# Five exchanges in a load queue: a v ahead of a q, and k and v ahead of weight blocks

## The chip, the cores and the metric

The kernel runs on one core of one Trainium2 chip. The metric is the device time of one execution in microseconds (us), taken as the median of several executions. A profiled execution gives a trace beside it. The engines of the core are called as in the profile: PE is TensorE (matrix products, with PEld for its weight loads), DVE is VectorE, ACT is ScalarE, POOL is GpSimd, and SP is SyncE, which here issues nearly all DMAs. PE writes into PSUM banks, DVE and ACT read them, and loads land in SBUF.

## The reference

Two stages follow each other. The first is a linear attention with decay, over 4 batches, 8 heads, 768 positions and a head dimension of 64, in blocks of 64 positions:

```python
intra = np.einsum('bhic,bhjc->bhij', qb, kb) * Dmask[None]
intra = np.einsum('bhij,bhjd->bhid', intra, vb)
inter = np.einsum('bhid,bhde->bhie', qb * lam_pow[None], kv_state)
out[:, :, sl] = intra + inter
kb_dec = kb * rev_pow[None]
kv_state = lam_block[None, :, None, None] * kv_state + np.einsum('bhsd,bhse->bhde', kb_dec, vb)
```

Its output, with the heads side by side, is x, 3072 tokens by 512. The second stage is a pair of products with a leaky activation between them; w_in is 512 x 2048 and w_out is 2048 x 512, both given as 64-bit floats:

```python
h = x @ w_in
g = np.maximum(0.01 * h, h)
return (g @ w_out).astype(np.float32)
```

## The kernel before

**Tiling.** The attention goes in 24 chunks of 128 positions (two blocks of the reference each), six to a batch, numbered 0 to 23 here. For a chunk c the kernel loads kc, qc and vc (`load_kq`, line 476, and `load_v`, line 538). A k or a q is two DMAs of 128 KB, a v one of 256 KB. All three have 256 bytes in a piece, one head of one position. PE transposes k and q with four products each (`transposes`, line 560), ACT or DVE copies the result out of PSUM (line 541), and POOL or DVE multiplies k by the decay (line 601). PE then makes the products of k and v (`kv` in `scores`), which renew the state, the scores (`go` in `scores`), and the output in three parts (`outputs`: `own`, then `inter(0)` and `inter(1)`). All of these are 64 x 64 products with line 420. Between the two `inter` parts stands a copy of two columns (`seen_po`, line 692), which orders them. The output goes to x in a split into three float32r parts: xh (line 708), xl (716) and xm (734).

For chunks 8 and 9 q isn't transposed on PE. It is loaded in 16 small pieces (`load_subs`, line 523, 32 KB each) into a buffer that DVE transposes (`turn`, line 532); DVE must have all 16 pieces first.

**Weights.** w_in goes in eight blocks of 256 columns. Each block is loaded in two halves of 512 KB (`to_float32`, line 797, called W below) into one of three buffers raw0 to raw2. ACT reads a half three times (lines 809, 811 and 813), DVE makes float32 of it (815, 816), and ACT or DVE splits the block into three parts wh, wm and wl (`parts`, 822, 825, 827). `up` (line 863) multiplies four chunks of x with a block, three products for the three parts; ACT applies the activation (890), and the result is stored to a buffer G in device memory (893). After all 24 chunks, `down` (929) reads G and multiplies with w_out.

**What sets the order.** A planner records every operation with a number, in the order in which Python calls come. `ORDER` (line 266) is a list written out in full: pairs of an operation's number and its engine. It fixes the order in which each engine gets its operations, 1,291 of 1,841 of them; the planner places the others behind the list by its own times. Each engine runs its own list strictly in order, so an operation that waits holds all that stand behind it on that engine; for SP this means all DMAs behind a waiting one.

```python
for i, e in self.order:
    if i < 0:
        done.append((free[e], len(done), i, e))
        free[e] -= 0.11 * i
        continue
    take(max(free[e], since(i, e)), i, e)
```

PSUM banks for an operation are handed out in the same order: `Slot("bank")` gets, of the banks pt, b10, b11 and b2 that are free at that point of the list, the one that was used last the longest ago (`resolve`):

```python
able = [x for x in self.kinds[s.kind] if holds[x] is None or not holds[x].left]
s.name = self.kinds[s.kind][s.fixed] if s.fixed is not None else min(able, key=lambda x: ended[x])
```

So moving an operation of PE can rename banks behind it. Which buffer a load writes is fixed by the chunk: even chunks use k0, q0, v0 and odd ones k1, q1, v1, so a load of chunk c + 2 waits until chunk c has been read. Chunks 2 and 3 have places of their own (k and v of 2 in gs0, of 3 in gs1, q of 3 in raw2).

The operations that this case speaks of:

| number | what | engine |
|---|---|---|
| 51 | load of v2 | SP |
| 73 | load of q3 (two DMAs, into raw2) | SP |
| 76 | transposes of q3 | PE |
| 59 | products of k2 and v2 | PE |
| 230, 224 | second and first half of w_in block 3 | SP |
| 135, 162, 121, 187 | load of k6, store of a part of G, load of v5, load of q7 | SP |
| 331 | second half of w_in block 4 | SP |
| 154 | load of v6 | SP |
| 268, 281, 280, 278 | four of the 16 pieces of q for chunks 8 and 9 | SP |
| 275 | the last of these pieces | SP |
| 208, 283, 303 | loads of v7, k8 and v8 | SP |
| 304 | load of k9 (two DMAs) | SP |
| 355 | second half of w_in block 7 | SP |

Of the kernel before, what the change touches and what calls it, by code (L numbers as in the profile page):

```python
# [239 lines left out]
def kernel(  # L240
# [127 lines left out]
    plan = Plan(kinds, also, {"k@2": early[0], "v@2": early[0], "k@3": early[1], "v@3": early[1], "q@3": early[2]})  # L368
    plan.fill, plan.idle, plan.warm, plan.order = busy, None if ORDER else busy, 1.3 + 0.22 * WARM, ORDER
    add = plan.add  # L370
# [685 lines left out]
```

## Time and profile before

| what | value |
|---|---|
| median of 3 runs | 607.72 us (606.0 to 608.35) |
| the profiled execution | 606.76 us, its span 605.0 us |
| busy, share of the span: PE | 597.4 us, 99% |
| DVE, ACT, POOL | 295.6 us (49%), 209.0 us (35%), 71.4 us (12%) |
| granted TensorE clock | 1.000 |
| DMA, mean over the span | 174 GB/s |

A row of the timeline reads: start in us from the span's start, length, engine, line, operation, written tile <- read tiles, partitions x elements, number of instructions merged into the row, and in brackets the idle time ahead of it with what ended that. Tiles go by the program's names: `att` is the common buffer of the attention's k, q, v and states, `raw` a weight half, `b`, `pt`, `po` and `psc` are PSUM banks, `gs` the staging of G. SPq rows are issues of DMAs; their length is that of the issue and not of the transfer. An issue that lasts longer than about half a microsecond was held while the queue took it in.

### The profile page before, as it was taken

To read this page: it belongs to the slowest core of one execution; us is meant where nothing else is said; L and a number is where in the kernel's file an instruction comes from. 1 tells how busy PE (TensorE), PEld (TensorE's weight loads), DVE (VectorE), ACT (ScalarE), POOL (GpSimd) and SP (SyncE) were. 2 spreads that over 40 slices of the span, in tenths; PEclk is the share of its full clock that TensorE was granted. 3 is DMA by queue.
4 is the path that set the end of the run, shared out by engine and by line. 5 is a ranking of instruction groups with operands and counts; after the bars stand their busy time and mean duration, and the time that the engine had idled before them with its cause. 6 is when DMAs were issued, how large, how long until landed. Compare 5 with 4: busy or idle time off the path is not lost.

```text
span 605.0 us, 12719 instructions
## 1 busy us (share of the span) xinstructions
PE 597.4 (99%) x5362; PEld 492.9 (81%) x5362; DVE 295.6 (49%) x410; ACT 209.0 (35%) x322; POOL 71.4 (12%) x85
## 2 busy tenths in 40 slices
PE   8899999999999999999999999999999999999997
PEld 6788888888888888887888888888888888888886
DVE  6898754350454434344166755354353543534430
ACT  3776651212433433435334421222312313214111
POOL 3321232241322031140000000000000000000000
PEclk9999999999999999999999999999999999999999
DMA  9998887598888788664875833424333333433201
GB/s 211 226 264 223 216 246 199 89 251 191 215 227 206 226 240 243 174 205 178 326 262 183 304 105 126 153 94 137 117 117 127 117 128 122 125 102 123 86 1 69
DMA packets 149993, 105.18 MB, mean 174 GB/s; under 512 B 125872, under 2 KB 126640, under 8 KB 149936
## 3 DMA queue, kind: packets, MB, share of 16 engines
q1 hardware_dynamic: 149648, 104.30, 59.5%
q8 instruction: 42, 0.69, 0.5%
q14 instruction: 15, 0.12, 0.1%
q10 hardware_dynamic: 288, 0.07, 0.0%
HBM read 68.69 MB, written 35.65 MB: 172 GB/s over the span
## 4 chain that ended last, share of the span: by engine, by line
PE 95%; DMA 3%; ACT 1%; issue 0%; DVE 0%; POOL 0%; SPq 0%; DVEq 0%; POOLq 0%; ACTq 0%
PE b L863 32%; PE b L929 16%; PE psc L929 11%; PE po L929 11%; PE pt L863 11%; PE pt L929 5%; PE po L420 4%; PE psc L420 3%; DMA att<-in_v_dram 1%; DMA att<-in_k_dram 1%; PE b L359 1%; DMA raw<-in_moe_w_in_dram 1%; PE b L560 1%; PE b L420 0%; PE pt L359 0%
## 5 line engine op out<-in xcount | busy, mean ns | idle before, releaser
L911 DVE SCALAR_TENSOR_TENSOR xl<-att,xh 128x1024 fp32r<-128x1024 f32 x48 | 58.7, 1222 | 125.8 <-ACT xh L910 125.8
L910 ACT ACTIVATE xh<-att 128x1024 fp32r<-128x1024 f32 x48 | 50.9, 1061 | 147.5 <-PE po L929 72.9
L863 PE MATMUL b<-xl,wl 128*128 128x512 f32 (+1 forms) x292 | 77.1, 389 | 0.0
L863 PE MATMUL b<-xh,wh 128*128 128x512 f32 (+1 forms) x292 | 76.5, 389 | 0.6 <-ACT wh L822 0.6
L863 PE MATMUL b<-xm,wm 128*128 128x512 f32 (+1 forms) x292 | 75.9, 390 | 0.0
L890 ACT ACTIVATE gs<-b 128x512 f32<-128x512 f32 x72 | 42.1, 597 | 94.8 <-PE b L863 86.3
L863 PEld LDWEIGHTS b<-xh,wh 128*128 128x128 f32 x292 | 53.9, 188 | 11.8 <-ACT wh L822 0.7
L863 PEld LDWEIGHTS b<-xl,wl 128*128 128x128 f32 x292 | 54.1, 188 | 11.2
L863 PEld LDWEIGHTS b<-xm,wm 128*128 128x128 f32 x292 | 53.8, 188 | 11.2
L913 DVE SCALAR_TENSOR_TENSOR xm<-xl,xh 128x1024 fp32r<-128x1024 f32 x48 | 58.8, 1226 | 4.7
L929 PE MATMUL b<-wh,xh 128*128 128x512 f32 x144 | 56.0, 389 | 0.0
L929 PE MATMUL b<-wl,xl 128*128 128x512 f32 x144 | 56.0, 389 | 0.0
L929 PE MATMUL b<-wm,xm 128*128 128x512 f32 x144 | 56.0, 389 | 0.0
L663 POOL TENSOR_TENSOR att<-att 128x256 f32<-128x256 f32 x40 | 28.0, 701 | 112.6 <-DVE att L660 59.9
L929 PE MATMUL psc<-wm,xm 128*128 128x512 f32 (+1 forms) x100 | 38.2, 387 | 0.0
L929 PE MATMUL po<-wm,xm 128*128 128x512 f32 (+1 forms) x100 | 37.9, 384 | 0.0
L929 PE MATMUL psc<-wh,xh 128*128 128x512 f32 x96 | 37.3, 389 | 0.0
L929 PE MATMUL psc<-wl,xl 128*128 128x512 f32 x96 | 37.3, 389 | 0.0
L929 PE MATMUL po<-wh,xh 128*128 128x512 f32 x96 | 37.3, 389 | 0.0
L929 PE MATMUL po<-wl,xl 128*128 128x512 f32 x96 | 37.3, 389 | 0.0
L420 PEld LDWEIGHTS po<-att 64*64 64x64 f32 x1408 | 26.9, 134 | 10.2 <-issue 8.2
L420 PE MATMUL po<-att 64*64 64x64 f32 x1408 | 33.0, 222 | 1.4 <-issue 0.9
(106 smaller groups left out, 863.9 us busy)
## 6 DMA issues: line engine op xcount, KB each, us to landing
att<-g SPq DMA_DIRECT2D x48, 512.0 KB, 3.4
g<-gs SPq DMA_DIRECT2D x47, 512.0 KB, 3.6
raw<-in_moe_w_in_dram SPq DMA_DIRECT2D x16, 512.0 KB, 5.9
raw<-in_moe_w_out_dram SPq DMA_DIRECT2D x16, 512.0 KB, 4.5
out_dram<-gs SPq DMA_DIRECT2D x23, 256.0 KB, 2.0
att<-in_k_dram SPq DMA_DIRECT2D x44, 128.0 KB, 3.9
att<-in_v_dram SPq DMA_DIRECT2D x22, 256.0 KB, 4.2
wo<-w SPq DMA_DIRECT2D x8, 512.0 KB, 4.3
```

The lines of the kernel that those rows point to most:

```text
L359: nc.tensor.matmul(wide[:, :k, :], lhsT=ident, rhs=_bc(ident[:, 0:C2], 1, k), start=True, stop=True, skip_group_check=True)
L420: nc.tensor.matmul(dst[HALF[cols]], lhsT=lhsT[HALF[rows]], rhs=rhs[HALF[rows]], start=start, stop=True, skip_group_check=True)
L560: nc.tensor.transpose(out=at[y], in_=src[:, 2 * y:2 * y + 2, :].rearrange("p a d -> p (a d)"), identity=ident)
L663: add("POOL", 0.62, lambda new=new, j=j: behind(("s", j), nc.gpsimd.tensor_tensor(state[(j + 1) % 4], new, _bc(lam_c, 2, D), op=ALU.mult)) ...
L863: nc.tensor.matmul(dst, lhsT=w[z][:, kk * 2 * P + f * P:kk * 2 * P + (f + 1) * P], rhs=x[z][:, kk, toks], start=start and kk == 0, stop=kk ...
L890: add("ACT", ns, lambda b=b, r=r: nc.scalar.activation(out=r(), in_=b(), func=AF.Prelu, bias=0.0, scale=1.0, alpha=0.01), [kb], [kg], rank ...
L910: add("ACT", 1.05, lambda: nc.scalar.activation(out=h, in_=graw[j], func=AF.Copy, bias=0.0, scale=NEAR), reads, wr("h"))
L911: add("DVE", 1.215, lambda: nc.vector.scalar_tensor_tensor(l, graw[j], 1.0, h.bitcast(F32), op0=ALU.mult, op1=ALU.subtract), reads + [f"rh ...
L913: add("DVE", 1.215, lambda: nc.vector.scalar_tensor_tensor(m, l.bitcast(F32), -S, h.bitcast(F32), op0=ALU.mult, op1=ALU.add), [f"rh{j}", f ...
L929: nc.tensor.matmul(to[:, cols], lhsT=ring[j][z][:, f * T + tb * P:f * T + (tb + 1) * P], rhs=W[pp][z][:, f * d_model:(f + 1) * d_model][:, ...
```

## The change

`ORDER` alone changes. Seen from the queue of SP there are five exchanges; on PE operation 76 moves behind 59. In the diff, other entries of the list are left out where the line is only "...", and each pair of lines is one place of the list.

```diff
-    (38, "DVE"), (73, "DMA"), (37, "DVE"),
+    (38, "DVE"), (37, "DVE"),
...
-    (51, "DMA"), (97, "ACT"), (104, "ACT"), (96, "ACT"), (171, "DMA"),
+    (51, "DMA"), (97, "ACT"), (104, "ACT"), (96, "ACT"), (73, "DMA"), (171, "DMA"),
...
-    (155, "PE"), (76, "PE"), (47, "DVE"), (77, "ACT"), (60, "DVE"), (59, "PE"), (65, "PE"),
+    (155, "PE"), (47, "DVE"), (77, "ACT"), (60, "DVE"), (59, "PE"), (76, "PE"), (65, "PE"),
...
-    (230, "DMA"), (135, "DMA"), (162, "DMA"),
+    (135, "DMA"), (162, "DMA"),
...
-    (187, "DMA"), (137, "PE"), (139, "PE"), (224, "DMA"),
+    (187, "DMA"), (137, "PE"), (139, "PE"), (230, "DMA"), (224, "DMA"),
...
-    (245, "PE"), (331, "DMA"), (232, "ACT"),
+    (245, "PE"), (232, "ACT"),
...
-    (234, "DVE"), (228, "DVE"), (271, "DMA"),
+    (234, "DVE"), (228, "DVE"), (331, "DMA"), (271, "DMA"),
...
-    (325, "DMA"), (268, "DMA"), (236, "DVE"), (281, "DMA"), (196, "ACT"), (201, "DVE"), (208, "DMA"),
-    (250, "PE"), (199, "ACT"), (261, "PE"), (204, "DVE"), (251, "ACT"), (280, "DMA"), (237, "DVE"), (278, "DMA"), (334, "ACT"), (283, "DMA"),
+    (325, "DMA"), (236, "DVE"), (196, "ACT"), (201, "DVE"), (208, "DMA"),
+    (250, "PE"), (199, "ACT"), (261, "PE"), (204, "DVE"), (251, "ACT"), (237, "DVE"), (334, "ACT"), (283, "DMA"),
...
-    (326, "ACT"), (267, "DMA"),
+    (326, "ACT"), (268, "DMA"), (281, "DMA"), (280, "DMA"), (278, "DMA"), (267, "DMA"),
...
-    (355, "DMA"), (304, "DMA"),
+    (304, "DMA"), (355, "DMA"),
```

1. The load of v2 goes ahead of the load of q3 (two DMAs). The transposes of q3 on PE go behind the products of k2 and v2, and the banks pt, b10 and b11 change names for the operations behind, up to the end of `up`; the order of the operations on PE, DVE, ACT and POOL is otherwise the same.
2. The second half of w_in block 3 goes behind the loads of k6, v5 and q7 and a store of G, six DMAs in all, to just ahead of that block's first half.
3. The load of v6 goes ahead of the second half of w_in block 4.
4. Four pieces of q go behind the loads of v7 and k8.
5. The load of k9 goes ahead of the second half of w_in block 7.

2 lines of the change are left out of this document (1 added, 1 removed).

## The prediction

> **What bounds the kernel now.** I read the page's first part, then the busy time by stage, then the timeline of TensorE and of the load queue in the first 70 us.
>
> ```profile
> span 605.0 us, 12719 instructions
> ...
> PE 597.4 (99%) x5362; PEld 492.9 (81%) x5362; DVE 295.6 (49%) x410; ACT 209.0 (35%) x322; POOL 71.4 (12%) x85
> ```
> ```profile
> 0.00:69.44 69.44, 65.34 (x1267) 52.60 (x1267) 55.70 (x104) 42.39 (x73) 19.14 (x29) 1.00 0.93 229
> 69.44:600.00 530.56, 530.52 (x4093) 439.03 (x4088) 239.10 (x305) 165.98 (x248) 52.24 (x56) 1.00 0.56 167
> ```
>
> In the stage rows the columns are the stage, its length and then the busy time of PE, weight loads, DVE, ACT and POOL, with the granted clock, the DMA share and the GB/s last. The reader is to see that TensorE (PE) is busy for 530.52 of 530.56 us from 69.44 on, at clock 1.00. All edits lie ahead of that. Behind it the work is the same and PE is full, so the change is worth as many microseconds as PE reaches the place now at 69.44 earlier or later. Ahead of it PE idles 69.44 - 65.34 = 4.1 us. That caps a gain at about 4 us, while a loss has no cap in these rows. The DMA engines are 0.93 busy in that stage, so the load queue is the second resource that matters.
>
> **The change part by part.** No instruction is added or removed. Five groups of issues change places in SyncE's queue (SP), the four transposes of q3 change places with the products of k2 and v2 on PE, and PSUM banks pt, b10 and b11 change names among the same uses. For the banks I take 0: each new owner still waits for a reader that ended earlier on ACT or DVE. A letter with a number is a chunk's load (v5), W is half a block of w_in.
>
> *First exchange, v2 ahead of q3.*
>
> ```profile
> 15.13 1.05 SPq L476 DMA_DIRECT2D raw<-in_q_dram  x2
> 16.23 0.51 SPq L538 DMA_DIRECT2D gs<-in_v_dram  x1
> ```
> ```profile
> 20.89 0.60 PE L560 MATMUL pt<-att,raw 128*128 128x128 f32 x4
> 21.59 0.69 PE L420 MATMUL b<-gs 64*64 64x64 f32 x32
> ...
> 23.75 0.46 PE L420 MATMUL po<-att 64*64 64x64 f32 x16
> ```
> ```profile
> 22.95 0.70 ACT L809 ACTIVATE w<-raw 128x512 f32<-128x512 f32 x1 [0.84 <-DMA raw<-in_moe_w_in_dram]
> 23.55 0.14 ACT L692 COPY att<-po 128x2 f32<-128x2 f32 x1
> ```
>
> v2 is issued 16.23 - 15.13 = 1.1 us earlier, q3 0.5 us later (v's issue of 0.51). The products, at 21.59 today, can follow their predecessor at 20.89, 0.7 us earlier, and the transposes (0.60) follow them. But the last part of this chunk's output, at 23.75, needs the small copy at 23.55 on ACT, and that stands behind an operation that waits for a W until 22.95. That W keeps its place. So PE is early and then waits: 0 gained from 23.75 on. If v2 is no earlier, 0 lost; if W is late too, up to 0.7 lost. I take 0.
>
> *Second, W (block 3) behind k6, the store of G01, v5 and q7 (six DMAs).*
>
> ```profile
> 31.56 0.46 SPq L797 DMA_DIRECT2D raw<-in_moe_w_in_dram  x1
> 33.52 0.92 SPq L476 DMA_DIRECT2D att<-in_k_dram  x2
> 35.19 0.59 SPq L538 DMA_DIRECT2D att<-in_v_dram  x1
> 35.84 3.50 SPq L476 DMA_DIRECT2D att<-in_q_dram  x2
> 39.43 0.74 SPq L797 DMA_DIRECT2D raw<-in_moe_w_in_dram  x1
> ```
> ```profile
> 39.39 0.73 PE L560 MATMUL po<-att 128*128 128x128 f32 x4
> ...
> 41.32 1.09 PE L420 MATMUL psc<-att 64*64 64x64 f32 x46 [0.35 <-DMA att<-in_v_dram]
> ```
> ```profile
> 41.47 0.81 ACT L811 ACTIVATE low<-raw 128x512 uint16<-128x512 uint32 x1
> 42.80 0.60 ACT L708 ACTIVATE xh<-po 128x512 fp32r<-128x512 f32 x1 [0.52 <-PE po L420]
> ...
> 45.91 0.79 ACT L811 ACTIVATE low<-raw 128x512 uint16<-128x512 uint32 x1 [0.83 <-DMA raw<-in_moe_w_in_dram]
> ```
>
> k6 waits for the chunk 4 products and can't be issued before 33.52 in either order. What changes is that 512 KB of W no longer lie ahead of it. v5 then lands ahead of W, and the 0.35 us wait at 41.32 goes. The four transposes of k6 take 0.73 where those of q3 above take 0.60, another 0.13. W goes out at 39.43 - 2.5 (the issue of q7 shrinks from 3.50 to about 1) = 36.9 instead of 31.56, and lands between 36.9 + 4.2 = 41.1 (the time that the W of 60.37 below takes) and 36.9 + 6.5 = 43.4 (that of the W of 39.43, which ACT gets at 45.91); I take 42. Its reader on ACT, at 41.47, waits about 0.6 us, and the next in that queue, xh at 42.80, slips to about 43. The bank that xh empties is next written by the transposes of k7, whose load is issued only behind the products at 41.32, so I take 0 for that. Gain 0.35 + 0.13 = 0.48 us; ends 0 (W still shares the engines) and 0.6.
>
> *Third, v6 ahead of a W (block 4); fourth, four pieces of transposed q behind v7 and k8.*
>
> ```profile
> 57.80 0.80 PE L560 MATMUL po<-att 128*128 128x128 f32 x4
> ```
>
> The third gains 0: PE follows without a wait today, and v6 comes 0.5 us earlier in issue; it keeps the products covered when PE comes early. The fourth brings k8 four issues forward. Its transposes take 0.80 against 0.60, so 0.20 us gained. The pieces only have to be there for the DVE transposes at 67.22 below.
>
> *Fifth, k9 (two DMAs) ahead of a W (block 7).*
>
> ```profile
> 60.37 0.40 SPq L797 DMA_DIRECT2D raw<-in_moe_w_in_dram  x1
> 60.87 0.96 SPq L476 DMA_DIRECT2D att<-in_k_dram  x2
> 61.89 0.49 SPq L523 DMA_DIRECT2D att<-in_q_dram  x1
> 62.43 0.44 SPq L538 DMA_DIRECT2D att<-in_v_dram  x1
> ```
> ```profile
> 66.59 0.68 PE L560 MATMUL po<-att 128*128 128x128 f32 x4 [0.33 <-DMA att<-in_k_dram]
> 67.20 0.93 PE L420 MATMUL po<-att 64*64 64x64 f32 x48
> 67.95 1.32 PE L420 MATMUL psc<-att 64*64 64x64 f32 x64
> 69.09 0.41 PE L420 MATMUL po<-att 64*64 64x64 f32 x16
> ```
> ```profile
> 67.22 1.30 DVE L532 STREAM_TRANSPOSE att<-att 128x512 f32<-128x512 f32 x2 [2.25 <-DMA att<-in_q_dram]
> ```
> ```profile
> 64.53 0.67 ACT L809 ACTIVATE w<-raw 128x512 f32<-128x512 f32 x1 [0.66 <-DMA raw<-in_moe_w_in_dram]
> 65.74 0.74 ACT L813 ACTIVATE low<-raw 128x512 f16<-128x512 f32 x1
> 68.20 0.16 ACT L692 COPY att<-po 128x2 f32<-128x2 f32 x1 [1.71 <-PE po L420]
> ```
>
> k9 is issued at most 0.5 us earlier and has 512 KB less ahead of it: the wait of 0.33 goes, and 0.08 of the transposes (0.68 against 0.60). It waits for the chunk 7 products that read the same buffer, and may have to wait for them, so up to 0.5 of the earlier issue can be lost unless PE is early; the W, the q piece and v8 are now queued behind that wait. Gain 0.41.
>
> The PE-side sum is 0 + 0.48 + 0 + 0.20 + 0.41 = 1.1 us. It isn't kept whole, because other work is late next at the same place. (a) The last q piece, issued at 61.89, releases the DVE transposes at 67.22; their second one ends at 67.22 + 1.30 = 68.5, and the scores of chunk 8, the second half of the 64 at 67.95, need it. (b) v8, issued at 62.43, is read by the first half at 67.95. (c) W moves behind 256 KB of k and two issues (0.96), so it lands between 64.5 + 1.0 = 65.5 and 66.8; its three operations on ACT take 65.74 + 0.74 - 64.53 = 1.95 us and stand ahead of the small copy at 68.20, for which the last 16 products at 69.09 wait. The copy could start at 67.5 to 68.8. All three go by when the queue has drained, which moves the same bytes in either order. If that time stays, 0 of the 1.1 us is kept. It may come earlier, because the load of k7 waits for the chunk 5 products, which come 0.5 us earlier, and because k9 fills a stretch in which the queue starves:
>
> ```profile
> 60.40:62.00 1.60, 1.60 (x71) 1.45 (x64) 1.57 (x2) 1.14 (x3) 0.00 (x0) 1.00 0.60 62
> 62.00:66.00 4.00, 4.00 (x19) 3.17 (x17) 2.60 (x5) 3.34 (x7) 2.27 (x3) 1.00 1.03 260
> ```
>
> 62 GB/s against 260 is 1.6 x 198 = 317 KB, or 1.2 us at 260 GB/s; an estimate from these two rows. Between 0 and 1.1 I take half, 0.5 us. So the span becomes 605.0 - 0.5 = 604.5 us. The profiled execution took 606.76 us, its span and 1.76 around it; like that, 606.3. It lay 0.96 below the median of 607.72, and the mean of the four executions (607.72, 608.35, 606.0, 606.76) is 607.2. Minus 0.5 that is 606.7, and from the median 607.2; I forecast the middle, 607.0.
>
> **A rule weighed.** In these rows loads end in the order of their issue: W of 60.37 lets ACT go at 64.53, k9 of 60.87 lets PE go at 66.59. The Trainium skill, "DMA: Bandwidth & Descriptors", section "Queues, rings and completion order", says that descriptors are consumed in ring order on each engine, but that completion is not first in, first out for an issuing engine. By the first half the exchanges move the landings, as summed; were landings free of the order, no wait would go, and the time would be rival one's. The trace agrees with the first half.
>
> **The rivals.** *One: hidden anyway.* The waits go, but PE stands at the scores of chunk 8 until 68.5 as today, because (a) keeps its time. For it: the DVE row waits 2.25 us for a load. Against it: the starved stretch. Time: span 605.0, median 607.7.
>
> *Two: slower, W holds ACT.* W of block 7 lands late, and the small copy behind it holds PE. It decides from the point where W lands later than 69.09 - 0.16 - 1.95 = 67.0. A W in the crowded stretch is slower than this one: the W at 39.43 releases ACT only at 45.91 (row above, 6.5 us), and one of 6.5 us issued at 61.4 lands at 67.9, 0.9 us beyond the point; with a wait of 0.7 of its own in the first exchange, 1.6. Span 606.6, time 609.3. Against it: W took 64.53 - 60.37 = 4.2 us here.
>
> *Three: all is kept.* The queue drains 1.2 us earlier, and PE keeps 1.1: span 603.9, time 606.6 from the median.
>
> **How the numbers follow.** Forecast (0.2 to 0.9 us off) 0.45, rival one 0.25, rival two 0.18, rival three 0.12. A measurement of this kernel tells about 0.5% from no change, 3.0 us; the three runs shown spread over 2.35 us. No case reaches 3.0 us by its mechanism, so what lies beyond is the spread of the medians and a stall that I don't see: 0.04 faster, 0.06 slower, 0.90 within. The range takes rival three less 1.2 us of the runs' spread at the low end, 605.4, and rival two without its own spread at the high end, 609.3.
>
> **What would show it.** Right: no PE wait on a v or k load between 30 and 68 us; v5, k8 and k9 landing earlier; PE's last 16 products of chunk 7 starting at 68.2 to 68.9 instead of 69.09, with a DVE or ACT wait just ahead; and the stage behind as full as now. Wrong: new PE waits ahead of 69 us on ACT's small copy or on the DVE transposes, k9's issue held by the chunk 7 products, or any PE idle time behind 70 us.

## The result, and the profile after

The changed kernel takes 609.28 us (median of 22 executions, 606.42 to 613.73) against 606.94 us for the kernel before (22 executions). The ratio is 1.0041, with a 95% interval of 1.0029 to 1.0054. A second measurement of the same two kernels gave 1.0054 (1.0036 to 1.0073). So the change costs 2.3 to 3.3 us. The time lies inside the range and within half a per cent, as forecast, but the forecast had the sign wrong: it said 0.5 us faster. Single executions of 850 to 2,104 us (one each of e2, e6 and e12 below, and one of the kernel before) are left out of all medians and counts.

The traced execution is the shortest of the 22 (606.42 us), so its trace alone does not show the loss; what the others do is read below from repeats and from neighbours of this kernel. Busy time by stage, of the changed kernel (columns as in the prediction):

```profile
span 604.6 us, 12718 instructions
```
```profile
0.00:69.39 69.39, 64.60 (x1266) 51.72 (x1267) 55.24 (x104) 41.95 (x73) 19.09 (x29) 1.00 0.92 231
69.39:600.00 530.61, 530.61 (x4095) 439.09 (x4090) 238.89 (x305) 165.87 (x248) 51.84 (x56) 1.00 0.56 167
```

The place that was at 69.44 is now at 69.39, and behind it PE is as full as before. Timeline of PE, the changed kernel:

```profile
39.96 1.05 PE L420 MATMUL psc<-att 64*64 64x64 f32 x46
...
56.61 0.87 PE L560 MATMUL po<-att 128*128 128x128 f32 x4 [0.19 <-DMA att<-in_k_dram]
...
65.25 0.60 PE L560 MATMUL po<-att 128*128 128x128 f32 x4
65.78 0.93 PE L420 MATMUL po<-att 64*64 64x64 f32 x48
67.89 1.34 PE L420 MATMUL psc<-att 64*64 64x64 f32 x64 [1.18 <-DMA att<-in_v_dram]
69.05 0.41 PE L420 MATMUL po<-att 64*64 64x64 f32 x16
```

PE seems to come early as summed: the products of v5 start at 39.96 (41.32 before) without a wait, and the transposes of k9 at 65.25 (66.59 before), 1.34 us earlier. Then 1.18 us go into a new wait for v8, whose products start at 67.89, where they started before (67.95). But the 1.34 us are no larger than what one kernel differs by from trace to trace. A second trace of the kernel before (e2 below, an execution of 605.17 us) has none of the waits that the prediction added up:

```profile
40.42 1.05 PE L420 MATMUL psc<-att 64*64 64x64 f32 x46
...
56.73 0.60 PE L560 MATMUL po<-att 128*128 128x128 f32 x4
...
65.10 0.74 PE L560 MATMUL po<-att 128*128 128x128 f32 x4
```

The products of v5 start between 39.89 and 41.32 in the six traces without the second exchange and between 39.96 and 41.49 in the fourteen with it; the mean is 40.57 in both. So no gain on PE is shown; the new wait for v8 is what stays. Timeline of SyncE's queue, the changed kernel:

```profile
51.69 5.35 SPq L523 DMA_DIRECT2D att<-in_q_dram  x5
57.14 0.40 SPq L893 DMA_DIRECT2D g<-gs  x1
57.58 3.32 SPq L523 DMA_DIRECT2D att<-in_q_dram  x6
61.01 1.67 SPq L476 DMA_DIRECT2D att<-in_k_dram  x2
62.77 0.46 SPq L797 DMA_DIRECT2D raw<-in_moe_w_in_dram  x1
63.28 0.46 SPq L523 DMA_DIRECT2D att<-in_q_dram  x1
63.79 0.44 SPq L538 DMA_DIRECT2D att<-in_v_dram  x1
64.33 0.52 SPq L893 DMA_DIRECT2D g<-gs  x1
```

Two rows of the same view of the kernel before:

```profile
57.00 3.27 SPq L523 DMA_DIRECT2D att<-in_q_dram  x6
...
62.98 3.03 SPq L893 DMA_DIRECT2D g<-gs  x1
```

Six small pieces stood in a row before, from 57.00 on; five more now stand in front of them, and only the store of G00 lies between, from 51.69 to 60.90. v8 is issued at 63.79 instead of 62.43, though PE needs it 1.2 us sooner. The store of G02 behind v8 took 3.03 us to issue before, which I read as a full queue ahead of it; now it takes 0.52, which fits an empty one. By this reading the holds have moved ahead of v8. Stretches of 5 us, the kernel before and the changed one:

```profile
55.00:60.00 5.00, 5.00 (x55) 3.76 (x55) 3.69 (x8) 3.20 (x5) 0.31 (x1) 1.00 0.81 207
60.00:65.00 5.00, 5.00 (x108) 4.30 (x101) 4.57 (x7) 3.48 (x7) 1.96 (x3) 1.00 0.88 202
```
```profile
55.00:60.00 5.00, 4.79 (x123) 3.56 (x123) 3.46 (x7) 3.35 (x6) 0.62 (x1) 1.00 0.61 159
60.00:65.00 5.00, 5.00 (x38) 3.81 (x28) 4.24 (x6) 2.82 (x5) 1.86 (x3) 1.00 0.59 119
65.00:70.00 5.00, 3.82 (x137) 3.19 (x136) 2.55 (x5) 2.43 (x5) 1.46 (x2) 1.00 1.08 345
```

The last two columns tell it: from 55 to 65 the DMA engines are 0.6 busy instead of 0.8 to 0.9 and move (207 - 159 + 202 - 119) x 5 = 655 KB less, which has to be made up behind 65. At 345 GB/s that is 1.9 us, an estimate from these rows. Here too the trace matters: e2's trace of the kernel before moves 159 and 217 GB/s, so it is 490 KB against that one, all of it between 60 and 65.

A second sign stands in the executions themselves. The mean granted clock of PE was 1.000 in 9 of the 22 and 0.993 to 0.997 in 13. The 9 average 608.0 us, the 13 average 610.5, the kernel before 607.0. A clock of 0.997 over 607 us would be 1.8 us, an estimate.

### The profile page after: what moved, and what is told of

Read it like the earlier page. It is cut to its first block, busy times and chain, and to the rows that moved or that the text cites. A ratio compares the mean times of both kernels' runs of the same rounds, so it can differ in the third digit from the quotient of the medians.

```text
span 604.6 us, 12718 instructions
## 1 busy us (share of the span) xinstructions
PE 596.4 (99%) x5362; PEld 491.9 (81%) x5362; DVE 294.9 (49%) x410; ACT 208.4 (34%) x322; POOL 70.9 (12%) x85
## 4 chain that ended last, share of the span: by engine, by line
PE 94%; DMA 3%; DVE 1%; ACT 1%; issue 0%; SPq 0%; DVEq 0%; ACTq 0%
PE b L863 31%; PE b L929 16%; PE pt L863 12%; PE psc L929 11%; PE po L929 11%; PE pt L929 5%; PE po L420 4%; PE psc L420 3%; DMA raw<-in_moe_w_in_dram 1%; DMA att<-in_v_dram 1%; DMA g<-gs 1%; PE b L560 1%; DMA att<-in_lam_dram 0%; PE po L560 0%; DVE att L403 0%
## 5 line engine op out<-in xcount | busy, mean ns | idle before, releaser
L863 PE MATMUL b<-xl,wl 128*128 128x512 f32 (+1 forms) x288 | 75.1, 387 | 0.0
L863 PE MATMUL b<-xh,wh 128*128 128x512 f32 (+1 forms) x288 | 74.5, 385 | 0.6 <-ACT wh L822 0.6
L890 ACT ACTIVATE gs<-b 128x512 f32<-128x512 f32 x70 | 40.7, 596 | 84.4 <-PE b L863 71.7
L863 PEld LDWEIGHTS b<-xl,wl 128*128 128x128 f32 x288 | 52.7, 188 | 11.1 <-DVE wl L827 0.4
L863 PEld LDWEIGHTS b<-xm,wm 128*128 128x128 f32 x288 | 52.5, 188 | 10.8
```

The costliest lines, as they stand in the source:

```text
L863: nc.tensor.matmul(dst, lhsT=w[z][:, kk * 2 * P + f * P:kk * 2 * P + (f + 1) * P], rhs=x[z][:, kk, toks], start=start and kk == 0, stop=kk ...
L890: add("ACT", ns, lambda b=b, r=r: nc.scalar.activation(out=r(), in_=b(), func=AF.Prelu, bias=0.0, scale=1.0, alpha=0.01), [kb], [kg], rank ...
```

## The experiments

Three theories were put to the chip. A: PE idles, its clock falls for a while, and that is the loss. B: the loads land late, and the clock is a by-product. C, formed after the first four runs, says why they are late: the small pieces of q are bound by SyncE's issue. Each ratio is to the kernel before, measured beside it on the same chip. "Low clock" counts executions with a mean clock under 0.998.

| run | kernel | median us | ratio (95%) | low clock |
|---|---|---|---|---|
| e1 | changed, again | 609.85 | 1.0054 (1.0036 to 1.0073) | 3 of 6 |
| e2 | before, again | 606.15 | 0.9997 (0.9985 to 1.0010) | 0 of 11 |
| e3 | without 1 | 611.79 | 1.0072 (1.0047 to 1.0097) | 6 of 7 |
| e4 | without 5 | 608.75 | 1.0047 (1.0031 to 1.0063) | 8 of 12 |
| e5 | without 4 | 607.07 | 1.0004 (0.9992 to 1.0017) | 0 of 12 |
| e6 | 4 alone | 607.63 | 1.0011 (0.9994 to 1.0028) | 3 of 11 |
| e7 | changed + 2 fillers | 608.95 | 1.0041 (1.0023 to 1.0059) | 2 of 9 |
| e8 | changed, W early | 606.76 | 0.9994 (0.9984 to 1.0004) | 0 of 11 |
| e9 | 3 and 4 | 607.01 | 1.0011 (0.9996 to 1.0027) | 3 of 12 |
| e10 | 2 and 4 | 607.89 | 1.0012 (0.9996 to 1.0028) | 1 of 12 |
| e11 | changed, 4 pieces on ACT | 606.04 | 0.9987 (0.9973 to 1.0002) | 0 of 12 |
| e12 | without 4, 4 pieces on ACT | 608.71 | 1.0031 (1.0014 to 1.0048) | 2 of 11 |
| e13 | 2, 3 and 4 | 608.35 | 1.0035 (1.0020 to 1.0050) | 3 of 8 |
| e14 | before, 4 pieces on ACT | 605.78 | 0.9990 (0.9977 to 1.0003) | 0 of 12 |
| e15 | changed, ACT and W early | 606.49 | 0.9994 (0.9979 to 1.0008) | 0 of 12 |
| e16 | 1 alone | 605.86 | 1.0000 (0.9986 to 1.0014) | 0 of 12 |
| e17 | changed + 4 fillers | 609.54 | 1.0057 (1.0039 to 1.0075) | 0 of 9 |
| e18 | e11 again | 606.58 | 1.0006 (0.9988 to 1.0024) | 1 of 12 |

**Both kernels again (e1, e2).** No edit.

> The changed kernel once more, unchanged, for a trace of a typical execution: the traced one took 606.42 us, 2.9 below its median of 609.28. In 13 of its 22 executions the mean granted clock of TensorE was 0.993 to 0.997, in 9 it was 1.000; the first group averages 610.3 us, the second 608.0. Theory A, the clock: a thin stretch of TensorE work ahead of 70 us makes the clock drop for a few us; 0.0035 of 605 us is 2.1 us. Then a trace with a mean clock under 1 shows one stretch ahead of 75 us with a granted clock of 0.5 to 0.9 and nothing else behind, and the ratio is again 1.003 to 1.005. Theory B, late landings: the clock is a by-product, v8, the last q piece or the W of block 7 lands 2 to 3 us later than in the trace at hand, and the wait of 1.2 us at 66.6 is 3 to 4 us.

> The kernel before once more, unchanged, for its clock execution by execution. Theory A: 1.000 in all or nearly all executions, ratio 0.999 to 1.001, 606.9 us. Theory B: executions under 1.000 are as common here as in the changed kernel (about 6 in 10) and cost it nothing that sets the two apart.

The loss is there again, and the kernel before is itself again with no low clock. Of all executions of the kernel before that ran beside these experiments and have a clock on record, 4 of 140 are low; of the changed kernel, 16 of 28. So the clock belongs to the change. But it is not all: the changed kernel's executions at a full clock are still 1.0 us slower than the kernel before (608.0 against 607.0). The trace of e1 has no stretch with a lower clock ahead of 75 us and took 607.9 us; its starved stretch and its wait for v8:

```profile
60.00:65.00 5.00, 5.00 (x126) 4.39 (x126) 4.34 (x6) 3.08 (x6) 1.84 (x4) 1.00 0.59 129
```
```profile
69.26 1.45 PE L420 MATMUL psc<-att 64*64 64x64 f32 x64 [1.20 <-DMA att<-in_v_dram]
```

The same picture: a starved queue and a wait of 1.20 us for v8. All this lies 1.4 us later than in the first trace, but so do the products of v5 already (41.49 against 39.96): that difference comes from ahead of the fourth exchange. The expected wait of 3 to 4 us (theory B) did not show in this trace.

**One exchange undone (e3, e4, e5).**

```diff
 # e3: exchange 1 back (q3 ahead of v2)
-(155, "PE"), (59, "PE"), (76, "PE")
+(155, "PE"), (76, "PE"), (59, "PE")
...
 # e4: exchange 5 back
-(282, "DMA"), (304, "DMA"), (355, "DMA")
+(282, "DMA"), (355, "DMA"), (304, "DMA")
...
 # e5: exchange 4 back
-(208, "DMA"), (283, "DMA"), (268, "DMA"), (281, "DMA"), (280, "DMA"), (278, "DMA")
+(268, "DMA"), (281, "DMA"), (208, "DMA"), (280, "DMA"), (278, "DMA"), (283, "DMA")
```

(Only the moved entries are shown, without what lies between them; in e3 the load 73 goes back with its transposes.)

> The changed kernel with the first exchange undone (q3 and its transposes ahead of v2 and the products of k2 and v2, as before); exchanges two to five stay. If what costs the 2.3 us lies at the scores of chunk 8 (66 to 70 us; A or B there), nothing comes back: ratio 1.003 to 1.005, the same mix of clocks. If the first exchange thins TensorE's work between 15 and 25 us and the clock drops there, all comes back: ratio 0.998 to 1.001 and clocks of 1.000.

> The changed kernel with the fifth exchange undone (W of block 7 ahead of k9, as before); exchanges one to four stay. If the cost lies at the scores of chunk 8 and comes from W and v8 standing behind k9: ratio 0.998 to 1.001, clocks of 1.000, no wait of 1.2 us on v8 at 66.6. If it lies in the first 25 us: ratio 1.003 to 1.005 as with all five.

> The changed kernel with the fourth exchange undone: the four pieces of transposed q stand ahead of and between v7 and k8 again; exchanges one, two, three and five stay. Theory C, the queue: the fourth exchange puts v7 and k8 early, where the queue is full and holds the issue (3.37 us on one piece of q at 51.69 in the changed kernel), and leaves twelve small pieces in a row behind, which SyncE issues at one per 0.46 us, slower than the DMA engines move them: 129 GB/s in 60:65 against 202 before, so W of block 7, the last piece and v8 are issued 1.4 us later and land later. Then without the fourth: ratio 0.997 to 1.001, clocks of 1.000, over 190 GB/s in 55:65 and v8 no later than the products need it. Rival (the W blocks moved by the second and third exchanges are what is late): ratio still 1.003 to 1.006 and the wait of 1.2 us or more ahead of the scores of chunk 8 stays.

Undoing the first or the fifth brings nothing back. Undoing the fourth brings all of it back, and no low clock is left. In e4's trace another load is late: with W ahead of k9 again, PE waits for k9 and not for v8.

```profile
67.76 0.99 PE L560 MATMUL po<-att 128*128 128x128 f32 x4 [1.92 <-DMA att<-in_k_dram]
```

In these traces the fifth exchange only chooses which of the two loads PE waits for. The trace of e3 caught what a low clock is. Its stretches around the wait, and its PE timeline:

```profile
68.50:69.00 0.50, 0.40 (x22) 0.26 (x17) 0.50 (x3) 0.43 (x2) 0.00 (x0) 0.76 1.06 392
69.00:72.00 3.00, 3.00 (x52) 2.59 (x52) 1.94 (x5) 1.09 (x2) 0.00 (x0) 0.50 0.87 265
72.00:72.50 0.50, 0.50 (x3) 0.36 (x3) 0.50 (x2) 0.12 (x1) 0.00 (x0) 0.83 0.70 168
```
```profile
68.03 1.92 PE L420 MATMUL psc<-att 64*64 64x64 f32 x64 [1.93 <-DMA att<-in_v_dram]
69.73 0.65 PE L420 MATMUL po<-att 64*64 64x64 f32 x16
70.31 2.03 PE L863 MATMUL b<-xm,wm 128*128 128x512 f32 x4
72.18 1.07 PE L863 MATMUL pt<-xh,wh 128*128 128x512 f32 x4
```

The rows that follow the same work in the changed kernel:

```profile
69.39 1.20 PE L863 MATMUL b<-xm,wm 128*128 128x512 f32 x4
70.42 1.08 PE L863 MATMUL b<-xh,wh 128*128 128x512 f32 x4
```

PE waits 1.93 us for v8, and some 0.7 us after it has resumed the granted clock falls to 0.50. With the 0.76 and 0.83 at its edges it lasts 0.24 + 3.0 + 0.17 = 3.4 us. The same 64 + 16 + 4 matmuls take 72.18 - 68.03 = 4.15 us instead of 70.42 - 67.89 = 2.53: 1.6 us, which comes on top of the wait. The Trainium skill, "TensorE: Matmul & The Clock Gate", section "Part 1: The HAM clock gate", has this as a gate that halves the clock by windows of about 3.4 us that run free of the program; the rate and the length agree with these rows. It puts the fall after an idle window of that length, and here 1.9 us of idleness were enough.

The trace of e9 below has a second such fall, behind a wait of 1.59 us for k9. It starts about 1 us after PE resumed and lasts 3.4 us too, at 0.50 in each half microsecond from 68.0 to 71.0; one of these rows:

```profile
66.85 0.95 PE L560 MATMUL po<-att 128*128 128x128 f32 x4 [1.59 <-DMA att<-in_k_dram]
```
```profile
68.50:69.00 0.50, 0.50 (x29) 0.50 (x27) 0.50 (x2) 0.00 (x0) 0.44 (x1) 0.50 1.02 393
```

The length of the wait does not decide it: e4's 1.92 us above and 1.77 us in e13 passed without a fall.

The trace of e5, in the same places:

```profile
60.00:65.00 5.00, 5.00 (x98) 4.31 (x92) 4.11 (x6) 2.98 (x6) 2.05 (x3) 1.00 0.69 164
```
```profile
67.77 1.28 PE L420 MATMUL psc<-att 64*64 64x64 f32 x64 [0.37 <-DMA att<-in_v_dram]
```

164 GB/s is less than the 190 that I expected, but the wait for v8 is 0.37. The loss is gone in the median; how, this trace does not show. v8 is issued at 64.00, no earlier than in the changed kernel. It lands 3.6 us after its issue instead of 4.0, and PE comes to it 0.7 us later, having waited 0.82 for k8.

**The fourth alone, and in company (e6, e9, e10, e13, e16).** The kernel before with the named exchanges and no others.

> The kernel before with the fourth exchange alone. Theory C: the same starved stretch (under 150 GB/s in 60:65), a wait of 1 to 3 us ahead of the scores of chunk 8 or on k9, clocks of 0.997 in about half of the executions, ratio 1.003 to 1.007. Rival (second and third exchanges): ratio 0.999 to 1.001.

> The kernel before with the third and fourth exchanges alone. The fourth alone gave 1.0011 (0.9994 to 1.0028), all five 1.0041 and 1.0054, so the fourth costs its full price only beside another. Theory C1: its partner is the third, whose W (block 4) is moved between v6 and the pieces of q, into the full queue (3.0 us of held issue at 42.0 in the changed kernel): ratio 1.003 to 1.006, clocks of 0.997 in half of the executions. Theory C2: its partner is the second: ratio 1.000 to 1.002 here.

> The kernel before with the second and fourth exchanges alone. Theory C2 (with the W of block 3 behind k6, v5 and q7, TensorE runs ahead by 1.3 us from 40 us on while the issue of the queue stays bound, so it meets v8 sooner): ratio 1.003 to 1.006, clocks of 0.997 in half of the executions. Theory C1: 1.000 to 1.002.

> The kernel before with exchanges two, three and four. Alone or in pairs with the fourth none of them cost more than 1.0012; all five cost 1.0041 and 1.0054. If the price needs the second and the third together (both bring TensorE forward and both fill the queue ahead of the pieces of q): 1.003 to 1.007, clocks of 0.997 in half of the executions. If it needs the first or the fifth as well: 1.000 to 1.002.

> The first exchange alone, priced at 0 in the prediction. The changed kernel without it gave 1.0072 (1.0047 to 1.0097) in 7 executions against 1.0054 with it, so it may gain up to 0.002. If it does: 0.997 to 0.999. If what TensorE gains there is lost again at ACT's small copy or behind it, as the prediction had it: 0.9995 to 1.001.

The fourth is needed, and alone it costs little: 1.0011, and the same with either the second or the third (C1 and C2 both fell). With both it is 1.0035, close to all five. The border is not sharp: the intervals of e6, e9 and e10 reach 1.0027 to 1.0028, that of e13 begins at 1.0020, and their low clocks (7 of 35 against 4 of 140) say that a part of the loss may be there already. The traces of e6 and e10 don't bear out theory C's stretch under 150 GB/s (168 and 153 GB/s from 60 to 65), that of e9 does (103). The first alone is worth 0, as the prediction had it. Where the loss lands isn't fixed: in the trace of e13, with W of block 7 still ahead of k9, PE waits most for k9 (its row of the waits: total, times, longest):

```profile
PE po L560 <- DMA att<-in_k_dram: 2.5, 3, 1.8
```

Why the second and the third both have to be there is open. That they bring PE forward isn't shown (the mean start of v5's products is the same with and without the second); that they queue more bytes ahead of the pieces is only argued.

**Is it the issue? (e8, e11, e18, e14, e15, e12).** e8 puts the W of block 7 into the starved stretch. e11 lets ACT issue four of the late pieces (op 269 in its place, 273, 282 and 275 behind ACT's small copy 288). e18 is e11 again, e14 has this without any exchange, e15 has both mends, e12 has it without the fourth exchange.

```diff
 # e8
-(304, "DMA"), (355, "DMA")
+(304, "DMA")
...
-(267, "DMA"), (247, "DMA"), (274, "DMA")
+(267, "DMA"), (247, "DMA"), (355, "DMA"), (274, "DMA")
...
 # e11
-                        move(0.55, lambda o=o, z=z: nc.sync.dma_start(
+                        move(0.55, lambda o=o, z=z, w=(nm, c, y, a): (nc.scalar if w in ON_ACT else nc.sync).dma_start(
```

> The changed kernel with the W of block 7 (second half) issued in the middle of the twelve small pieces of q, behind the store of G00 at 57.5, instead of behind k9 at 62.8. Theory C: it fills the stretch in which the DMA engines starve, v8 and the last piece of q follow k9 directly and are issued about 0.5 us earlier with 512 KB less ahead of them, so they land 1.5 to 2 us earlier and the wait ahead of the scores of chunk 8 goes: ratio 0.996 to 0.999, clocks of 1.000, faster than the kernel before by the 1.1 us of the forecast's sum or more. Rival (total bytes set when v8 lands, whatever the order): the wait stays over 1 us and the ratio 1.003 or more.

> The changed kernel with four of the late small pieces of q (the last one among them) issued by ACT instead of SyncE: one ahead of the small copy at 59.3, three behind it, where ACT stands idle. Theory C (the pieces are bound by SyncE's issue, 0.46 us each): some 1.8 us of issue go from ahead of k9, W and v8, so v8 is issued 4 us or more ahead of its need instead of 2.3 to 2.8, the wait ahead of the scores of chunk 8 falls under 0.5 us, and the ratio is 0.997 to 1.001 with clocks of 1.000. Rival (the DMA engines are the bound, whoever issues): v8 lands as late as before relative to the products, ratio 1.003 or more.

> The changed kernel with four of the late pieces of q issued by ACT, once more, to halve its interval (0.9973 to 1.0002 the first time): 0.998 to 0.9995 if the gain over the kernel before is real, 1.000 to 1.001 if the first result was luck; under 1.002 in any case if the issue of SyncE is what the changed kernel lost by.

> The kernel before with the four pieces of q issued by ACT and no exchange, the control for the run in which the changed kernel gets them (0.9987). If four issues fewer on SyncE help whatever stands in the queue: 0.997 to 0.999. If they only mend what the fourth exchange broke: 0.999 to 1.001; and if k8 behind the pieces is now what is late (the version without the fourth exchange waited 1.8 us for it): 1.001 to 1.003.

> All five exchanges, four pieces of q issued by ACT, and the W of block 7 issued behind the store of G00 instead of behind k9: both mends together. If v8 was held by W ahead of it (issue of v8 held 61.09 to 62.93 and a wait of 0.4 us left in the trace with ACT's queue), it lands 1 us earlier: 0.997 to 0.9985, faster than the kernel before. If one mend takes all there is: 0.998 to 1.000.

> Exchanges one, two, three and five, without the fourth, and the same four pieces of q issued by ACT. If issue is what holds v8 (Theory C), this keeps the gain that the forecast summed: ratio 0.996 to 0.999, faster than the kernel before. If the drain of the queue by bytes sets the time (rival one of the prediction), 1.000 as without the fourth alone.

With four issues fewer on SyncE the changed kernel is back at the kernel before, twice: 0.9987 and 1.0006. The bytes are the same, and so are all products. The trace of e11, its stretch, its queues and its wait:

```profile
60.00:65.00 5.00, 5.00 (x37) 4.08 (x27) 3.52 (x6) 2.81 (x5) 2.27 (x3) 1.00 0.87 214
```
```profile
61.09 1.84 SPq L538 DMA_DIRECT2D att<-in_v_dram  x1
```
```profile
56.88 0.34 ACTq L523 DMA_DIRECT2D att<-in_q_dram  x1
59.31 1.33 ACTq L523 DMA_DIRECT2D att<-in_q_dram  x3
```
```profile
66.75 1.16 PE L420 MATMUL psc<-att 64*64 64x64 f32 x64 [0.40 <-DMA att<-in_v_dram]
```

The engines are fed (214 GB/s instead of 119), and v8 is at the queue at 61.09. The next table sets three things beside each other: the lead, by which v8's issue lies ahead of the moment when PE could take its products (their start less their wait for v8); the landing, the time from v8's issue to its arrival; and the wait.

| trace | v8 issued | lead, us | landing, us | wait for v8, us | ratio of the kernel |
|---|---|---|---|---|---|
| before | 62.43 | 67.95 - 62.43 = 5.5 | 5.3 | 0 | 1 |
| e2 | 61.16 | 66.52 - 61.16 = 5.4 | 5.1 | 0 | 0.9997 |
| e14 | 61.06 | 66.82 - 61.06 = 5.8 | 5.5 | 0 | 0.9990 |
| e18 | 61.02 | 66.34 - 61.02 = 5.3 | 5.2 | 0 | 1.0006 |
| e11 | 61.09 | 66.75 - 0.40 - 61.09 = 5.3 | 5.5 | 0.40 | 0.9987 |
| e6 | 63.78 | 67.78 - 0.29 - 63.78 = 3.7 | 3.9 | 0.29 | 1.0011 |
| e10 | 64.99 | 69.08 - 0.66 - 64.99 = 3.4 | 3.9 | 0.66 | 1.0012 |
| e5 | 64.00 | 67.77 - 0.37 - 64.00 = 3.4 | 3.6 | 0.37 | 1.0004 |
| e15 | 64.92 | 68.34 - 0.25 - 64.92 = 3.2 | 3.3 | 0.25 | 0.9994 |
| e8 | 66.35 | 69.66 - 0.70 - 66.35 = 2.6 | 3.2 | 0.70 | 0.9994 |
| e12 | 65.41 | 70.08 - 1.19 - 65.41 = 3.5 | 4.5 | 1.19 | 1.0031 |
| changed | 63.79 | 67.89 - 1.18 - 63.79 = 2.9 | 4.0 | 1.18 | 1.0041 |
| e1 | 65.03 | 69.26 - 1.20 - 65.03 = 3.0 | 4.1 | 1.20 | 1.0054 |
| e3 | 63.58 | 68.03 - 1.93 - 63.58 = 2.5 | 4.3 | 1.93 | 1.0072 |

Where the landing is longer than the lead, PE waits for the difference and 0.1 to 0.2 us more. (In e8 and e10 the profile names DVE as what ended the wait, but PE starts 0.1 to 0.2 us after v8 has landed.) In the table the kernels with 1.0012 or less wait 0.7 us or less for v8, those with 1.0031 or more wait 1.18 or more. Neither lead nor landing alone sorts them: a lead of 3.2 us was nearly enough in e15, where W goes out earlier, and 3.5 was not in e12. e8's row bears out how its mend works: nothing large stands right ahead of v8 there, and it lands in 3.2 us instead of 4.0 to 4.3, though the trace is of the longest of its executions (608.04 us). The rate from 60 to 65 us goes the same way: 164 GB/s and more in every trace of a kernel with a ratio of 1.0006 or less, 129 and less where it is 1.0031 or more; e9 with 103 GB/s and 1.0011 is the exception, and its trace is a long one among its executions (608.37 us, median 607.01).

Is it the issue, or the bytes that go to another queue? Four pieces are 128 KB, 0.6 us at 214 GB/s; four issues at 0.55 us are 2.2 us, and v8 goes out 63.79 - 61.09 = 2.7 us earlier. These are estimates and speak for the issue; no run holds the two apart. The Trainium skill, "DMA: Bandwidth & Descriptors", section "Rules for kernel authors", says that spreading DMAs over several issuing engines adds no bandwidth and only saves the sequencer's issue time. The second half agrees with e11 and e18, where the time saved was enough to take the loss away; no run here tests the first.

e14 and e15 say that the mends don't add up and give no sure gain over the kernel before: 0.9990 and 0.9994, both intervals with 1 in them. e12 contradicts both of its expectations, and theory C with them: four issues fewer on SyncE did not help there. Of PE's waits and of SyncE's:

```profile
PE po L560 <- DMA att<-in_k_dram: 1.8, 1, 1.8
```
```profile
SPq L476 <- PE psc L420: 1.7, 1, 1.7
```

The 1.8 are a wait for k8, which without the fourth exchange stands behind the pieces. PE is late by it, so that k9 may not be issued until the products of chunk 7 have read its buffer: SyncE stands idle for it (its next issue is at 62.02, the pieces ahead of it end at 60.45), W's issue then takes 2.31 us, and v8 stands behind both (65.41). So in this trace the queue is starved (129 GB/s) by a held load and not by the issue of pieces. Why k8 is so late isn't settled: up to its load the queue of e12 is that of e5, entry for entry, where PE waits 0.82 for it.

**The clock (e7, e17).** Filler matmuls on PE ahead of the products of k8 and v8, where PE waits for v8; e7 has two, e17 four. The diff is that of e17; e7 has -16 in place of -32.

```diff
-(310, "PE"), (311, "PE")
+(-32, "PE"), (310, "PE"), (311, "PE")
```

> The changed kernel with two filler matmuls (128x512 on the identity, into a free bank, some 1.8 us at full clock) on TensorE ahead of the products of k8 and v8, in the place where it waits for v8. If part of the loss is the clock (it falls to 0.50 for 3.4 to 4 us once TensorE has stood idle for some 2 us, as the trace without the first exchange shows at 68.9 to 72.9): no execution under 0.998, the slowest near 610 instead of 613.7, ratio 1.0015 to 1.003 against 1.004 to 1.0055. If the clock follows something else than the idle stretch (the run of small 64x64 products, say), executions of 0.997 stay as common and the ratio stays or grows by up to 0.001.

> The changed kernel with four filler matmuls (3.5 us, twice those of the first filler run) where TensorE waits for v8. They cover any wait that the traces show (1.2 to 2.1 us), so TensorE is never idle there. If the clock falls because TensorE is idle: no execution under 0.998; the time is set by the filler, 606.4 - 1.2 + 3.5 = 608.7 us, with a spread no larger than that of the kernel before. If it falls for another reason: executions of 0.997 stay at about half, and the median goes to 610 or more.

The rows of e17 on PE:

```profile
67.29 3.70 PE L359 MATMUL b<-att 128*128 128x512 f32 x8
70.92 1.16 PE L420 MATMUL psc<-att 64*64 64x64 f32 x64
```

Low clocks: 16 of 28 without filler, 2 of 9 with 1.8 us of it, 0 of 9 with 3.6 us. So it is idleness at this place that lowers the clock. The time does not improve (609.5 instead of the 608.7 that I worked out), since the filler stands where the wait stood; it only takes away the slowest executions (611.1 at most, 613.7 without). So theory A holds for the clock, as a consequence of late loads. B's late landings are there, but the clock is not a mere by-product: a fall costs 1.6 us in e3's rows, and about every second execution has one. C is the best account of why the loads are late, with e12 against it.

The mean loss of 2.5 us (2.3 between the medians) can be split by the clock. Executions at a full clock lose 608.0 - 607.0 = 1.0 us. Executions with a low clock are another 2.5 us slower, and 13 of 22 are such: 0.59 x 2.5 = 1.5 us. Of the 2.5, 1.6 are the slow matmuls if e3's rows are typical; that the rest is longer waits is not shown.

## Why the prediction was wrong

- **What bounds the kernel.** Right. Nothing changes behind 69.4; the stage behind is full in both.
- **First exchange, 0.** Right: 1.0000 alone.
- **Second, 0.48.** The wait for v5 is gone in the first trace, but in e2's trace the kernel before doesn't have it either, and v5's products start at 40.57 on average with and without this exchange. Its other side wasn't seen: with the third and the fourth it is part of the loss.
- **Third, 0.** Hardly a loss alone with the fourth (1.0011), but with the second and the fourth it makes one (1.0012 without it in e10, 1.0035 with it in e13).
- **Fourth, 0.20. This is the step that failed.** "The pieces only have to be there for the DVE transposes": I priced what the pieces are needed for, not what it costs to issue them. Moved together behind v7 and k8, they meet a full queue first (5.35 us for five) and an empty one then (3.32 us for six, at 119 GB/s), and k9, W, the last piece and v8 all stand behind them. The price of that is the loss: without the fourth the kernel is at 1.0004, and with four of the pieces issued by ACT at 0.9987 and 1.0006. k8 gained nothing for it: its transposes wait 0.19 us in the first trace, and in e2's trace of the kernel before they take 0.60, so that the 0.20 wasn't there to gain.
- **Fifth, 0.41.** PE doesn't wait for k9 in the traces with all five, but it doesn't in e2's trace of the kernel before either. It waits longest for k9 where the fourth is there without the fifth (1.92 us in e4, 1.59 in e9, 1.77 in e13). Without the fifth the loss stays (1.0047).
- **What is kept of the sum.** The 1.1 us were waits and slow transposes of one execution; e2's trace has none of the waits, so that they were no property of the kernel. I named v8 among three things that are late next, but took it that the queue drains at the same time "in either order", or earlier. It drained later: v8 landed between 67.8 and 70.2 in the four traces with that queue (changed, e1, e7, e17), between 66.3 and 67.7 in three with the order of before behind 20 us (before, e2, e16). The term was not 0 to 1.1 kept: executions at a full clock lost 1.0 us.
- **Rival one** (hidden anyway) describes the traced execution well: last products at 69.05 instead of 69.09, though v8 and not the DVE transposes is what holds them. **Rival two** had the right sign and, by luck, the right size (609.3): the load that held PE was v8, not W at ACT's copy. No case had the clock in it; at 1.6 us in 13 of 22 executions it would be about 1 us of the loss, an estimate from e3's rows.

## What to carry to other kernels

Many small loads in a row on one queue can be bound by the engine that issues them: here 0.46 to 0.55 us for each 32 KB, about 60 GB/s, while the DMA engines fell to 0.6 busy. Put large loads between them, or issue some from another engine that idles there, and price a moved load by what stands behind it on its queue: set the lead that each load has over its need beside the time that it takes to land (3.2 to 5.5 us for the same 256 KB here). A wait that one trace shows may not be there in the next execution, so take a second trace before you add such waits up. And a wait of PE can cost more than its length: after 1.6 to 1.9 us of idleness the clock halved for 3.4 us, in some executions and not in others, so compare the granted clock of all executions and not of one trace.

## What the runs showed of the hardware

- The granted clock fell to 0.50 for 3.4 us after PE had idled for 1.93 us (e3) and for 1.59 us (e9), not at once but 0.7 and 1.0 us after it resumed. After 1.92 us (e4) and 1.77 us (e13) it did not fall. The mean clock was low in 16 of 28 executions of the changed kernel and not in the others.
- A DMA issued by ACT took 0.34 to 0.44 us of its queue (three in 1.33 us). Of the kernels with four such issues, e11, e18, e14 and e15 were no slower than the kernel before (0.9987, 1.0006, 0.9990, 0.9994); e12 was (1.0031).
- The same 256 KB load (v8) took 3.2 to 5.5 us from its issue to its landing (e8, e15: 3.2 and 3.3; e11, e14: 5.5).
- One execution can mislead: the first trace of the changed kernel was 0.3 us faster than that of the kernel before, and the medians are 2.3 us apart the other way.
